# Attention with a float32 P turned by TensorE, and an order from a list scheduler, in a three-part kernel on one core

## The chip, the cores and the metric

The kernel runs on one core of one Trainium2 chip. The metric is the device time of one execution in microseconds (us); lower is better.

## What is computed

Three layers follow one another. The first is attention with rotary positions: 4 batches, 8 heads, 576 positions, 64 numbers a head. The second (called `moe` in the code) mixes each row with the row before it and squares a ReLU. The third (`moe2`) multiplies one half of a hidden layer by a normalised other half that was mixed over the positions.

```python
scores = scale * np.matmul(q_rot, k_rot.transpose(0, 1, 3, 2))
scores = scores - np.max(scores, axis=-1, keepdims=True)
attn = np.exp(scores)
attn = attn / (np.sum(attn, axis=-1, keepdims=True) + 1e-09)
attn_out = np.matmul(attn, v)
...
xk = mu_k * x + (1.0 - mu_k) * x_prev          # xr the same with mu_r
k = np.maximum(xk @ w_k, 0.0)
v = k * k @ w_v
x = v / (1.0 + np.exp(-(xr @ w_r)))
...
h = np.maximum(x @ w_in, 0.0)
u, v = h[..., :512], h[..., 512:]
v_n = (v - mean(v)) / np.sqrt(var(v) + 1e-06)
v_s = np.einsum('ts,bsd->btd', w_spatial, v_n) + b_spatial[None, :, None]
out = (u * v_s) @ w_out
```

## The kernel before

**Units of attention.** Heads go in pairs (16 of them, NP = 4 to a batch). A unit m is one block of 128 query rows of both heads of a pair; every fifth block of a pair has only 64 rows, and those of two pairs share a unit. So 72 units cover all, 18 to a batch; one in nine is such a shared unit. For each unit `scores` makes two PSUM tiles `s` (two banks each) by float32 products of `rot` (q and k after `rope`); each float32 product of the source shows as two MATMUL rows in the trace, so an ordinary unit has 8 rows and a shared one 16. Then come, for each of the two heads j: `top` (the negated row maximum, VectorE), `expo` (exp with row sums, ScalarE, into the float32 tile `pf`), and, after `norm` (1/sum), `high` and `low`, which write the normalised P as a float16 value and a float16 remainder (ScalarE and VectorE, tile `p`). `turn` transposes both by one DMA from SyncE (`pt<-p`). `values` multiplies the turned pieces with v, itself held as float16 value and remainder: 36 float16 products (72 in a shared unit) into `pv`. `gather` copies `pv` to the row tile `xt`, which is also stored to memory (`x_dram`).

**v before its use.** For each pair `v_max` takes the largest |v| (VectorE, then `partition_all_reduce` on GpSimd), `v_scale` makes scales from it, `v_split` the two float16 pieces, `v_copy` two moves by DMA. q and k are loaded through GpSimd's queue (L162).

**The first layer after attention.** Of each batch, and of each half h of its positions, `mix` makes the mixed input as two float32r pieces, `k_dot` 8 groups of 12 float32r products (tile `mk`), `k_square` the squared ReLU and its two pieces, `v_dot` 4 groups of 24 products (tile `mv`), `v_out` the copy and store to `v_dram`. That is 384 float32r products of 288 columns for a batch. The 16 pieces of the weights `w_k` and `w_v` arrive as 64-bit numbers, which `weight64` turns into float32r pieces by ScalarE, VectorE and GpSimd (L98 to L117).

**The second phase** (from L452 on) does the rest for the four batches (tiles `r`, `hv`, `u`, `sp`, `o`); its weights go through `weight64` too. Its pools open when the attention's and the first phase's close.

**Order.** An agenda of slots (two to a unit) and keys sets in which order the first phase is written out; the framework may still move instructions of an engine, as the trace shows for L223. The first `moe` work of a batch comes `LAG + 6` slots after the batch's last unit.

Of the kernel before, what the change touches and what calls it, by code (L numbers as in the profile page):

```python
# [11 lines left out]
F16 = mybir.dt.float16  # L12
# [6 lines left out]
NP = H // 2  # L19
# [4 lines left out]
NKC = 9  # L24
NFC = DF // 128
NX = NXV = 33
LATE_W = True
NFIRST = 2
WB, GB, WB2, GB2 = 5, 3, 3, 2
LAG = 8  # L30
EARLY = 0
PRE = 13
K_N, K_T, K_H, K_E, K_L = 1, 2, 3, 4, 5
K_M, K_V = 40, 10
RAW, ROT, PFS, P16S, PTS, XTS = 3, 6, 4, 3, 3, 6
P_SCALE = 2.0 ** 14


def raw(ap):
    return ap.bitcast(F32)  # L40


@with_exitstack
def body(ctx: ExitStack, tc, qp, kp, vp, cs, mu_k, mu_r, w_k, w_v, w_r, w_in, w_sp, b_sp, w_out, out):
# [8 lines left out]
    xpool = ph1.enter_context(tc.tile_pool(name="xpool", bufs=1))  # L53
    st0 = ExitStack()
    stage = [st0.enter_context(tc.tile_pool(name="st0", bufs=1)), WB, GB]
    att = ExitStack()
    at = att.enter_context(tc.tile_pool(name="att", bufs=1, side="right"))
    st0p = ExitStack()

    ps_x = st0p.enter_context(tc.tile_pool(name="ps_x", bufs=1, space=PSUM))  # L60
    ps_s = att.enter_context(tc.tile_pool(name="ps_s", bufs=2, space=PSUM, side="right"))
    ps_pv = att.enter_context(tc.tile_pool(name="ps_pv", bufs=1, space=PSUM, side="right"))
# [3 lines left out]


    cst = at.tile([128, 2, S], F32, name="cst")
    nc.sync.dma_start(cst, cs)

    mix4 = const.tile([128, NP, 4], F32, name="mix4")
    nc.sync.dma_start(mix4[:, :, 0], mu_k.rearrange("(c p) -> p c", p=128))
    nc.sync.dma_start(mix4[:, :, 2], mu_r.rearrange("(c p) -> p c", p=128))
    for k in (0, 2):
        nc.vector.tensor_scalar(mix4[:, :, k + 1], mix4[:, :, k], -1.0, 1.0, op0=ALU.mult, op1=ALU.add)
    epsc = const.tile([128, 2], F32, name="epsc")
    nc.vector.memset(epsc[:, 0:1], 1e-6)
    nc.vector.memset(epsc[:, 1:2], -0.5)
    warm = const.tile([128, 1], F32, name="warm")
    musc = const.tile([128, B, NP, 4], F32, name="musc")  # L80

    def new_stage(tag):
        n = 512 if tag != "ww" else 1160 if "p2" in pool else 1024
        return stage[0].tile([128, n], I32, tag=tag, bufs=stage[1 if tag == "ww" else 2], name=nc.get_next_instruction_name())

    def weight64(dram, r, hi, lo, c):  # L90
# [5 lines left out]
        def load():  # L96
            t["w"] = new_stage("ww")[:, :1024].rearrange("p (a b) -> p a b", b=2)
            nc.sync.dma_start(t["w"], src)  # L98

        def scale():  # L100
            lo, up = (t["w"][:, :, k] for k in range(2))
            t["g"] = t["x"] = new_stage("wg")
            nc.scalar.mul(t["g"].bitcast(F32), up.bitcast(F32), 2.0 ** -112)
            nc.scalar.mul(lo, lo.bitcast(U32), 2.0 ** -29)
            nc.vector.tensor_scalar(up, up, -2 ** 31, None, op0=ALU.bitwise_and)

        def shift():
            nc.vector.scalar_tensor_tensor(t["x"], t["g"], 3, t["w"][:, :, 1], op0=ALU.logical_shift_left,
                                           op1=ALU.bitwise_or)
# [3 lines left out]

        def low():
            x = t["x"].bitcast(F32)
            nc.scalar.copy(hi, x)
            nc.gpsimd.tensor_tensor(lo, x, raw(hi), op=ALU.subtract)  # L117

        return load, scale, shift, rest, low
# [15 lines left out]

    HEAD = slice(0, 64), slice(64, 128)

    agenda = []

    def add(slot, key, fn):  # L140
        agenda.append((slot, key, len(agenda), fn))

    def steps(gen, slots, key):
        for s in slots:
            add(s, key, lambda: next(gen, None))

    UN = 9 * NP
    preps = {}
    xt = {}

    def prep(i, s):

        b, p = divmod(i, NP)
        t = {}

        def load(which, part):
            if part == 0:
                t["raw", which] = at.tile([128, 2, S], F32, tag="raw", bufs=RAW, name=f"raw{i}_{which}")
            if i == 0:
                nc.sync.dma_start(t["raw", which][:, part, :], (qp, kp)[which][b, p, :, part, :])  # L160
            elif part == 0:
                nc.gpsimd.dma_start(t["raw", which], (qp, kp)[which][b, p])  # L162

        def rope(which):
            x = t.pop(("raw", which))
            y = t[which] = at.tile([128, S], F32, tag="rot", bufs=ROT, name=f"rot{i}_{which}")
            nc.vector.tensor_tensor(x, x, cst, op=ALU.mult)  # L167
            nc.vector.tensor_tensor(y, x[:, 0, :], x[:, 1, :], op=ALU.add)

        def v_load():  # L170
            t["vr"] = at.tile([128, 10, D], F32, tag="vr", bufs=1, name=f"vr{i}")
            nc.sync.dma_start(t["vr"], vp[b, p])

        def v_max():
            vm = t["vm"] = at.tile([128, 4], F32, tag="vm", bufs=2, name=f"vm{i}")
            nc.vector.tensor_reduce(vm[:, 0:1], t["vr"], axis=AX.XY, op=ALU.max, apply_absolute_value=True)
            nc.gpsimd.partition_all_reduce(vm[:, 1:2], vm[:, 0:1], channels=128, reduce_op=bass_isa.ReduceOp.max)
# [195 lines left out]
    def moe1(b, s):  # L373
# [5 lines left out]
        for h in range(2):  # L379
            for fc in range(NFC):  # L380
# [5 lines left out]
                if fc % 2:  # L386
                    steps(g, (m + 2,), 1.6)
# [293 lines left out]
```

## Time and profile before

| | |
|---|---|
| median of 3 runs | 937.1 us (934.18 to 942.13) |
| profiled execution: span from first to last instruction | 938.4 us |
| TensorE (PE) busy with matmuls | 796.6 us, 85% |
| VectorE (DVE), ScalarE (ACT), GpSimd (POOL) busy | 583.1, 464.0, 144.0 us |
| mean granted TensorE clock | 0.921 of 2.4 GHz |
| DMA packets under 512 bytes | 172705 of 198321 |

For the profiled execution no time beside its span is listed. A busy PE is not a PE at its peak, since rows of matmuls overlap; rates are read from how many rows start in a stretch.

### The profile page before, as it was taken

The page shows a single profiled execution, that of the slowest core. Times are in us where ns is not written, and L with a number is a line of the kernel's source. Part 1 is how long each engine was busy: PE and PEld are TensorE (multiplying, and loading weights), DVE is VectorE, ACT ScalarE, POOL GpSimd, SP SyncE. Part 2 cuts the span into 40 slices and gives each one's busy share as a digit, 9 for nine tenths or more (in the row PEclk, how much of TensorE's full clock was granted, in tenths as well). Part 3 has the DMA queues.
Part 4 walks back from the last instruction along what each step waited for, and adds up shares of the span by engine and source line. Part 5 has one row for each costly group of instructions (what it writes and reads, how often), then busy time and mean ns, then how long its engine had stood idle before and what let it go on. Part 6 is the DMA issues. An engine that isn't in the chain of part 4 may idle for free. (4 is left out here: it accounts for less than half of the span.)

```text
span 938.4 us, 16942 instructions
## 1 busy us (share of the span) xinstructions
PE 796.6 (85%) x6872; PEld 663.8 (71%) x6872; DVE 583.1 (62%) x1031; ACT 464.0 (49%) x900; POOL 144.0 (15%) x185
## 2 busy tenths in 40 slices
PE   1322478766999999898999999999989999999998
PEld 1111245444677776686777878998979999999998
DVE  3667496676688685687686785596485633254401
ACT  1525365545565563565675775576273442253311
POOL 1525360000000000000000000246160100010000
PEclk9999756557599999899999999999999999999999
DMA  7449587676497689777766758543532020200001
GB/s 277 150 113 149 137 171 133 153 164 157 88 186 177 110 152 128 145 169 167 139 115 149 147 116 139 156 142 127 167 119 77 1 101 13 89 14 26 26 27 51
DMA packets 198321, 114.20 MB, mean 122 GB/s; under 512 B 172705, under 2 KB 176801, under 8 KB 198242
## 3 DMA queue, kind: packets, MB, share of 16 engines
q1 hardware_dynamic: 191618, 90.69, 44.7%
q0 software_dynamic: 4320, 17.70, 6.4%
q10 hardware_dynamic: 2304, 4.73, 1.7%
q8 instruction: 54, 0.88, 0.4%
q14 instruction: 25, 0.20, 0.1%
HBM read 52.26 MB, written 14.16 MB: 71 GB/s over the span
## 5 line engine op out<-in xcount | busy, mean ns | idle before, releaser
L223 PE MATMUL s<-rot,rot 64*128 64x288 f32 (+1 forms) x640 | 200.7, 516 | 107.8 <-ACT pf L235 92.3
L223 PEld LDWEIGHTS s<-rot,rot 64*128 64x128 f32 (+1 forms) x640 | 103.5, 214 | 159.2 <-ACT pf L235 108.4
L235 ACT ACTIVATE pf<-s,sm 128x576 f32<-128x576 f32 x144 | 106.1, 738 | 100.2 <-DVE sm L230 93.9
L277 PEld LDWEIGHTS <-vv 128*64 128x64 f16 x2880 | 92.5, 123 | 60.1 <-issue 59.2
L251 DVE SCALAR_TENSOR_TENSOR p<-pf,sm,p 128x576 f16<-128x576 f32 x144 | 115.8, 829 | 30.5 <-ACT p L247 30.1
L247 ACT ACTIVATE p<-pf,sm 128x576 f16<-128x576 f32 x144 | 103.7, 767 | 46.9 <-DVE sm L241 17.3
L277 PE MATMUL pv<-pt,vv 128*64 128x128 f16 (+1 forms) x2880 | 109.7, 235 | 20.0 <-DMA pt<-p 20.0
L335 PE MATMUL mk<-x,wk 128*128 128x288 f32 x768 | 121.6, 307 | 3.1 <-DVE rl L346 2.8
L335 PEld LDWEIGHTS mk<-x,wk 128*128 128x128 f32 x768 | 106.2, 192 | 19.1 <-issue 8.6
L364 PE MATMUL mv<-kh,wv 128*128 128x288 f32 x512 | 116.4, 310 | 0.0
L230 DVE TENSOR_REDUCE sm<-s 128x1 f32<-128x576 f32 x144 | 106.5, 748 | 11.1 <-PE s L223 11.0
L364 PEld LDWEIGHTS mv<-kh,wv 128*128 128x128 f32 x512 | 86.8, 194 | 10.7 <-issue 8.4
L364 PE MATMUL mv<-kl,wv 128*128 128x288 f32 x256 | 77.7, 304 | 1.4 <-DVE kl L352 1.4
L167 DVE TENSOR_TENSOR raw<-raw,cst 128x1152 f32<-128x1152 f32 x32 | 44.2, 1383 | 40.3 <-DMA raw<-qp 25.2
L452 PE MATMUL r<-xr,wr 128*128 128x288 f32 x384 | 55.9, 301 | 3.3 <-DVE xr L456 2.5
L452 PEld LDWEIGHTS r<-xr,wr 128*128 128x128 f32 x384 | 53.4, 193 | 4.4 <-DVE xr L456 2.9
L452 PE MATMUL sp<-ws,vn 128*128 128x288 f32 x384 | 53.9, 295 | 0.0
L452 PE MATMUL o<-g,wo 128*128 128x288 f32 x384 | 53.0, 296 | 0.5 <-ACT os L582 0.5
L452 PE MATMUL u<-x,wi 128*128 128x288 f32 x384 | 53.2, 296 | 0.0
L452 PEld LDWEIGHTS u<-x,wi 128*128 128x128 f32 x384 | 52.4, 188 | 0.9
L452 PEld LDWEIGHTS sp<-ws,vn 128*128 128x128 f32 x384 | 52.4, 188 | 0.7
L452 PEld LDWEIGHTS o<-g,wo 128*128 128x128 f32 x384 | 51.7, 188 | 1.4 <-ACT os L582 1.2
(325 smaller groups left out, 973.8 us busy)
## 6 DMA issues: line engine op xcount, KB each, us to landing
raw<-kp POOLq DMA_DIRECT2D x15, 576.0 KB, 7.5
raw<-qp POOLq DMA_DIRECT2D x15, 576.0 KB, 6.1
vr<-vp SPq DMA_DIRECT2D x16, 320.0 KB, 3.6
xd<-xt ACTq DMA_DIRECT2D x16, 288.5 KB, 4.6
vd<-vs SPq DMA_DIRECT2D x32, 144.0 KB, 1.8
v<-vd SPq DMA_DIRECT2D x16, 288.0 KB, 2.8
out<-os SPq DMA_DIRECT2D x16, 288.0 KB, 2.1
vv<-vv SPq DMA_DIRECT2D x32, 128.0 KB, 2.9
```

Of the source, the lines that this page charges most:

```text
L167: nc.vector.tensor_tensor(x, x, cst, op=ALU.mult)
L223: nc.tensor.matmul(o, q[r, 128 * c:min(128 * c + 128, S)], k[r, h * HALF:(h + 1) * HALF], start=True, stop=True)
L230: nc.vector.tensor_reduce(sm[:, 0, j:j + 1], ps[j], axis=AX.XY, op=ALU.max, negate=True)
L235: nc.scalar.activation(pf[j].rearrange("p (a b) -> p a b", a=2), ps[j], AF.Exp, bias=sm[:, 0, j:j + 1], scale=1.0, accum_out=sm[:, 1, j:j ...
L247: nc.scalar.mul(p16[:, j, 0, :], pf[j], sm[:, 3, j:j + 1])
L251: nc.vector.scalar_tensor_tensor(p16[:, j, 1, :], pf[j], sm[:, 3, j:j + 1], p16[:, j, 0, :], op0=ALU.mult, op1=ALU.subtract)
L277: nc.tensor.matmul(o, preps[i]["vv"][:, kc, j, D * hl:D * hl + D], a, start=kc + hl == 0, stop=kc + hl == NKC)
L335: nc.tensor.matmul(ps[:, :HALF], wk[w][:, c, fc * 128:(fc + 1) * 128], a[:, c, :], start=m == 0, stop=m == 11)
L364: nc.tensor.matmul(ps[:, :HALF], wv[w][:, fc, dc * 128:(dc + 1) * 128], a, start=m == 0, stop=m == 23)
L452: nc.tensor.matmul(ps[:, h, :HALF], w, a[:, h * HALF:(h + 1) * HALF], start=m == 0, stop=m == n - 1)
```

## The change

P stays float32 and is not divided by its row sum before it is turned. TensorE turns it with an identity matrix, 4 blocks of 128 columns into one PSUM bank (`turn`, n = 0 and 1, one for each head) and a last block of the two heads' remaining columns together with the broadcast reciprocals of the sums (n = 2). `take` copies these three to SBUF, two on ScalarE and one on VectorE. `values` is then 10 float32 products of 64 by 128 with the unsplit v, and `gather`, now on VectorE, multiplies by the turned reciprocals while leaving PSUM. In shared units P is normalised first (`scaled`) and `gather` copies. v's maximum, scales, split and moves go, and with them `partition_all_reduce` and the `musc` scales. q and k are loaded by SyncE, `v_out` moves to ScalarE, the square of the ReLU becomes one product of 576 columns for two groups.

The whole first phase, the weights, and the first loads and weights of the second phase become steps of a `Plan`: each has an engine, an estimated duration, dependencies and a rank, and `order` takes at each point the step that can begin first. It is written out in that order, which nothing moves afterwards. Scores of a unit are one step for both heads, with the heads' products alternating, and wait for both exps of the unit before. The moe products go in pieces of 6. Two PSUM banks are shared by moe products and `values` (`m`), two serve `turn`. The buffers of weights go from 5 and 3 to 3 and 2, and the second phase has 4 instead of 3 of the PSUM tiles of `hv`.

```diff
+    def order(self):
+        free = dict.fromkeys(("PE", "ACT", "DVE", "POOL", "SP"), 0.0)
...
+                for s in steps:
+                    if any(d.end is None for d in s.deps):
+                        continue
+                    t = max([free[e]] + [d.end + d.after for d in s.deps])
+                    if s.take:
+                        if not room[s.take]:
+                            continue
+                        t = max(t, min(room[s.take])[0])
+                    key = (t, s.rank)
...
-            nc.gpsimd.partition_all_reduce(vm[:, 1:2], vm[:, 0:1], channels=128, reduce_op=bass_isa.ReduceOp.max)
...
-                nc.gpsimd.dma_start(t["raw", which], (qp, kp)[which][b, p])
...
+                    nc.sync.dma_start(t["raw", k], (qp, kp)[k][b, p])
...
+    plan = Plan({"m": 2, "t": 2, "ww": WB, "wg": GB})
...
+        def scaled(u):
+            p = st["p"][:, u, :]
+            nc.vector.tensor_scalar(p, p, st["r"][:, u, 0:1], None, op0=ALU.mult)
+
+        def turn(n, slot):
+            pt = st["t", n] = ps_t.tile([128, 4, 128], F32, tag=f"t{slot}", name=f"t{m}_{n}")
+            p = st["p"]
...
+            elif n < 2:
+                for c in range(4):
+                    k = 64 * n + 128 * c
+                    nc.tensor.transpose(pt[:, c, :], p[:, n, k:k + 128], ident)
+            else:
+                nc.tensor.transpose(pt[:, 0, :], p.rearrange("p a b -> p (a b)")[:, 512:640], ident)
+                nc.tensor.transpose(pt[:, 1, :], st["r"].rearrange("p a b -> p (a b)"), ident)
...
+            nc.scalar.copy(o, x) if eng == "ACT" else nc.vector.tensor_copy(o, x)
...
+                for c in range(5):
+                    for j in range(2):
...
+                            a, x = (v[:, 4 * j + c, :], pt[:, 4 * j + c, :]) if c < 4 else \
+                                (v[HEAD[j], 8, :], pt[HEAD[j], 8, :])
+                        nc.tensor.matmul(o, a, x, start=c == 0, stop=c == 4)
...
+                nc.vector.tensor_tensor(rows(i)[:, 1 + 128 * c:129 + 128 * c], st["v"][:, 0:128], st["pt"][:, 9, :],
+                                        op=ALU.mult)
...
+        scored[m] = s = add("PE", 1.95 if tail else 1.0, scores, need + [exps.get((m - 1, j)) for j in range(2)], m - 1.0)
+        mx = [add("DVE", 0.75, lambda j=j: top(j), [s], m - 0.6) for j in range(2)]
...
+            turned[m, n] = add("PE", (0.4, 0.4, 0.25, 0.1)[n], lambda slot, n=n: turn(n, slot), ready[n], m + 0.1 * n, take="t")
+            eng = ("ACT", "ACT", "DVE", "DVE")[n]
...
+        v = valued[m] = add("PE", 1.0, values, ev + [vloads[i] for i, _ in w], m + 0.9, take="m")
...
+            z = add("PE", 0.79, lambda slot, k_dot=k_dot: k_dot(0, slot), done + wk_ready, rank(fc), take="m")
+            p = add("PE", 0.79, lambda k_dot=k_dot: k_dot(1), [z], rank(fc) - 1)
...
-        nc.vector.tensor_copy(vs, ps[:, :HALF])
+                nc.scalar.copy(vs, xs["v", dc][:, :HALF])
...
+    close = add("SP", 0.0, open_second, over, 74, 0.1)
...
+    with tc.manual_schedule():
+        plan.emit()
...
-    ps1 = ctx.enter_context(tc.tile_pool(name="ps1", bufs=3, space=PSUM, reuse_waits="tile"))
+    ps1 = ctx.enter_context(tc.tile_pool(name="ps1", bufs=4, space=PSUM, reuse_waits="tile"))
```

## Rows read from the trace of the kernel before

**Rows 1.** The page: span and busy us (share of the span) of each engine.

```profile
span 938.4 us, 16942 instructions
...
PE 796.6 (85%) x6872; PEld 663.8 (71%) x6872; DVE 583.1 (62%) x1031; ACT 464.0 (49%) x900; POOL 144.0 (15%) x185
```

**Rows 2.** Windows of all engines: stretch, its us, busy us (instructions) each, clock, DMA.

```profile
15.00:190.00 175.00, 91.53 (x666) 56.93 (x667) 117.44 (x184) 84.29 (x165) 58.31 (x53) 0.78 0.65 146
...
400.00:570.00 170.00, 165.15 (x1766) 130.20 (x1760) 130.31 (x255) 107.66 (x226) 7.00 (x17) 0.99 0.69 141
570.00:669.00 99.00, 94.51 (x886) 90.39 (x883) 64.41 (x102) 55.89 (x109) 35.65 (x27) 1.00 0.49 132
```

**Rows 3.** The same windows, of L223 (scores) alone: PE and PEld.

```profile
15.00:190.00 175.00, 66.90 (x162) 33.94 (x163) 0.78 0.65 146
...
400.00:570.00 170.00, 54.62 (x232) 28.68 (x232) 0.99 0.69 141
```

**Rows 4.** Waits from 15 to 190 us: in total, times, longest.

```profile
PE s L223 <- ACT pf L235: 63.2, 15, 16.7
...
PE pv L277 <- DMA pt<-p: 20.0, 4, 13.1
...
ACT I-587_588 L103 <- POOL wk L117: 14.4, 1, 14.4
```

**Rows 5.** Timeline of POOL: start, us, what, idle before it.

```profile
58.62 0.38 POOL L177 PARTITION_ALL_REDUCE vm<-vm  x1 [6.03 <-DMA I-618_619<-w_v]
...
67.90 1.25 POOL L117 TENSOR_TENSOR wk<-I-364_365,wk 128x512 fp32r<-128x512 f32 x1 [8.28 <-issue]
```

**Rows 6.** Timeline of PE near the end of attention, at full clock.

```profile
564.95 1.24 PE L223 MATMUL s<-rot,rot 64*128 64x288 f32 x8
566.12 0.40 PE L364 MATMUL mv<-kh,wv 128*128 128x288 f32 x1
...
567.90 1.20 PE L277 MATMUL pv<-pt,vv 128*64 128x128 f16 x36
569.03 1.24 PE L223 MATMUL s<-rot,rot 64*128 64x288 f32 x8
```

**Rows 7.** Timeline of all engines from 428 us: scores of one head alone.

```profile
427.88 1.23 PE L223 MATMUL s<-rot,rot 64*128 64x288 f32 x4
```

**Rows 8.** Single lines: ns of one row (min/median/max), first and last start.

```profile
L223 PE MATMUL s<-rot,rot x640: 402/403/846, 15.2 to 569.9; 64*128 64x288 f32 x128, 64*64 64x288 f32 x32
...
L277 PE MATMUL pv<-pt,vv x2880: 196/219/317, 57.1 to 594.0; 128*64 128x128 f16 x152, 128*64 128x64 f16 x40
...
L335 PE MATMUL mk<-x,wk x768: 289/295/610, 247.5 to 654.5; 128*128 128x288 f32 x192
```

**Rows 9.** Groups by line and shape: count, busy us, mean ns, idle before.

```profile
L251 DVE SCALAR_TENSOR_TENSOR p<-pf,sm,p 128x576 f16<-128x576 f32 x144 | 115.8, 829 | 30.5 <-ACT p L247 30.1
L230 DVE TENSOR_REDUCE sm<-s 128x1 f32<-128x576 f32 x144 | 106.5, 748 | 11.1 <-PE s L223 11.0
...
L235 ACT ACTIVATE pf<-s,sm 128x576 f32<-128x576 f32 x144 | 106.1, 738 | 100.2 <-DVE sm L230 93.9 <-DVE p L251 4.7 <-DVE sm L241 1.2
L247 ACT ACTIVATE p<-pf,sm 128x576 f16<-128x576 f32 x144 | 103.7, 767 | 46.9 <-DVE sm L241 17.3 <-ACT pf L235 15.3 <-issue 11.4
...
L235 ACT ACTIVATION_READ_ACCUMULATOR pf<-s,sm 128x1 f32 x144 | 27.9, 194 | 0.0
...
L291 ACT COPY xt<-pv 128x512 f32<-128x512 f32 x16 | 9.2, 574 | 3.1 <-PE pv L277 3.1
```

**Rows 10.** Timeline of PE: the first phase's last product and the second's start.

```profile
668.10 0.29 PE L364 MATMUL mv<-kh,wv 128*128 128x288 f32 x1
668.23 6.41 PE L452 MATMUL r<-xr,wr 128*128 128x288 f32 x48
```

**Rows 11.** Windows 570 to 669 us: PE, PEld and ACT of `r`; PE and PEld of `mk`.

```profile
570.00:669.00 99.00, 8.90 (x54) 7.86 (x55) 1.30 (x2) 1.00 0.49 132
...
570.00:669.00 99.00, 42.14 (x288) 38.78 (x288) 10.81 (x24) 9.62 (x24) 1.00 0.49 132
```

More of the change, by code (lines that the diff above doesn't have):

```diff
@@ L433, in body @@
[L433 to L439 removed]
+        return [(2 * g, 4), (2 * g + 1, 4)] if w == 4 else [(2 * g + w // 5, w % 5 if w < 4 else w - 5)]
@@ new lines, in body @@
+    for c in range(16):
+        k = c < 8
+        args = (w_k, c // 2, wk[0][:, c // 2], wk[1][:, c // 2], c % 2) if k else (w_v, c - 8, wv[0][:, c - 8], wv[1][:, c - 8], 0)
+        (wk_ready if k else wv_ready).append(weight_steps(lambda args=args: args, 1.1 * c + (0 if k else 6)))
+    for m in range(NU):
+        for i, _ in which(m):
+            while i not in ropes:
+                prep(len(vloads))
+        unit(m)
+        for i in range(B * NP):
+            if i not in ropes and i >= ROT // 2 and max(which_last(i - 3)) <= m:
+                prep(i)
+        if m % 18 == 17:
+            if m == NU - 1:
+                over = list(plan.steps)
+            for h in range(2):
+                feed(m // 18, h)
@@ new lines, in body, with open_second @@
+    second = {}
+    st2 = ExitStack()
+    def open_second():
+        att.close()
+        p2 = second["p2"] = ctx.enter_context(tc.tile_pool(name="p2", bufs=1, side="right", reuse_waits="tile"))
+        second["wr"] = [p2.tile([128, NP, DM], F32R, tag=f"wr{i}", name=f"wr{i}") for i in range(2)]
+        second["wi"] = [p2.tile([128, NP, DF], F32R, tag=f"wi{i}", name=f"wi{i}") for i in range(2)]
+        second["xr"] = [p2.tile([128, NP, S], F32R, tag=f"xr{i}", name=f"xr{i}") for i in range(2)]
+        stage[:] = st2.enter_context(tc.tile_pool(name="st2", bufs=1, side="right", reuse_waits="tile")), WB2, GB2
@@ new lines, in mix_steps, with load, parts, first @@
+    def mix_steps(c, r, old):
+        t = {}
+        def load(slot):
+            t["x"] = new_stage("ww", slot).bitcast(F32)
+            nc.sync.dma_start(t["x"][:, :S + 1], x_dram[0][:, c, :])
+        def parts():
+            x = t["x"]
+            return x[:, :S], x[:, 1:S + 1], x[:, S + 1:2 * S + 1], second["xr"][0][:, c, :], second["xr"][1][:, c, :]
+        def first():
+            a, _, y, _, _ = parts()
+            nc.scalar.mul(y, a, mix4[:, c, 3:4])
+        def then():
+            _, a, y, _, _ = parts()
+            nc.vector.scalar_tensor_tensor(y, a, mix4[:, c, 2:3], y, op0=ALU.mult, op1=ALU.add)
+        def high():
+            _, _, y, hi, _ = parts()
+            nc.scalar.copy(hi, y)
+        def low():
+            _, _, y, hi, lo = parts()
+            nc.vector.tensor_tensor(lo, y, raw(hi), op=ALU.subtract)
+        s = x = add("SP", 0.4, load, [old], r - 1, 3.5, take="ww")
+        for eng, us, fn in (("ACT", 0.7, first), ("DVE", 0.75, then), ("ACT", 0.7, high)):
+            s = add(eng, us, fn, [s], r)
+        add("DVE", 0.75, low, [s], r, give=x)
@@ L614, in body @@
         gate(b)
-        if b == 0 and not LATE_W:
-            more_weights()
-            st2.close()
-            p4 = ctx.enter_context(tc.tile_pool(name="p4", bufs=1, side="right", reuse_waits="tile"))
         if b % 2:
```

631 lines of the change are left out of this document (325 added, 306 removed).

## The prediction

> **What bounds the kernel now.** The page comes first: PE is busy for 85% of the span [rows 1]. That is an average over stages with different limits, so the windows by stage come next, then the waits and the timeline inside each. The scores line serves as the clock of the first phase: 18 units show 160 of its rows (16 ordinary units of 8, two shared ones of 16).
>
> From the first scores at 15.2 us [rows 8] to 190 us the trace has 162 rows, so 18 units take 175 us, 9.7 us each [rows 3]. There PE is busy for half of the time, at a mean granted clock of 0.78, VectorE for two thirds, ScalarE for half [rows 2]: nothing is full, and the chain stalls. The waits name its links [rows 4]: scores wait 63.2 us for exps, up to 16.7 us at once; products with v wait 20 us for the transposing DMA; ScalarE once stands 14.4 us behind a weight step of GpSimd. The timeline of POOL shows why GpSimd was late: around the partition_all_reduce, 0.38 us of work, it sits idle for 6.03 us before and, after one DMA issue, 8.28 us "issue" behind it [rows 5]. ScalarE executes in order, so exps stand behind a weight step that waits for GpSimd, and scores behind the exps.
>
> The last scores start at 569.9 us [rows 8]; so the other 54 units take 380 us, 7.0 us each. From 400 to 570 us PE is busy for 165.15 of 170 us [rows 2]; 232 score rows at 8.9 a unit are 26.1 units, 6.5 us each [rows 3]. This stage is bound by PE. Its bill for a unit: scores 54.62 / 26.1 = 2.09 us; products with v 1.13 us, from one group's start to the next's (567.90 to 569.03) [rows 6]; moe 384 / 18 = 21.3 products at 1.78 / 12 = 0.148 us (566.12 to 567.90) [rows 6], 3.16 us. Sum 6.38, against 165.15 / 26.1 = 6.33.
>
> From 570 to 669 us PE still does the 288 + 288 moe products left over (the `mk` row shows 288; the `mv` ones are the other half, as the split of 8 groups of 12 and 4 of 24 makes equal) and 54 of `r` [rows 11]. The second phase proper runs from 668.23 us to the end, 270 us [rows 10, 1].
>
> **Part by part: PE in the stage that it bounds.** Scores: the four rows of one head alone occupy 1.23 us [rows 7], the eight of both heads 1.24 us, 1.17 to the next group [rows 6]. Two heads side by side cost what one does. Before, the framework mostly kept them apart (2.09 us a unit); the change writes them alternating, nothing moves them, and both tiles are awaited first. So 1.17, and with eight more rows in a shared unit, 1.28 on average: 0.81 less.
>
> A float32 row of 288 columns shows 402 ns, a float32r row 295 [rows 8]; float32r rows start every 6.41 / 48 = 0.134 us [rows 10], so I estimate 0.134 + 0.107 = 0.24 us for a float32 row. Four of these are 0.96, which leaves 0.21 of the 1.17 as the change-over between kinds of products. For 128 columns the float32 row is 0.107 us.
>
> Products with v: 10, so 20 rows, in pairs that use different halves of the output. Pairs do run together: the 36 float16 rows take 1.13 us, 0.031 each, while 128 columns alone at the float32r rate are 0.060. So 10 x 0.107 + 0.21 = 1.28 us, 0.15 more; ends 1.13 (nothing dearer than now) and 2.35 (no pairing).
>
> Turning is new on PE and no row shows it: 10 blocks of 128 by 128 a unit. Lower end 0.060 us each, one pass of 128 columns; upper end 0.214, a full float32 product, two rows. Within one pass, loading 128 columns of weights is hidden in the 0.134 us of a float32r product, so it costs at most that. I take the middle of 0.060 and 0.134, 0.095, since each block is loaded as weights and used once, and one change-over: 1.15 us. With three change-overs the ends are 0.8 and 2.77.
>
> The page "TensorE: Matmul & The Clock Gate", Part 4, of the Trainium skill puts one such transpose at some 275 ns inside a kernel, though for bf16. No row here is a transpose; the float16 rows with v last 219 ns each [rows 8] and yet follow every 31, so a row's length isn't its price in a stream. By that figure the sum would be 1.8 us a unit more and the whole near 995 us.
>
> Moe keeps its products: 3.16 us. Sum 1.28 + 1.28 + 1.15 + 3.16 = 6.9 us a unit, against 7.0 now. What pairing gives, turning takes. 54 x 6.9 = 373 us.
>
> The other engines have room under 6.9 us. VectorE now has 130.31 / 26.1 = 5.0 us a unit, ScalarE 107.66 / 26.1 = 4.1 [rows 2]. VectorE loses two `low` of 0.829 [rows 9] and the work on v, and gains a copy, the scaling gather and a broad reciprocal, each at most the 0.574 of a copy of 512 columns [rows 9]: about 4 to 5. ScalarE loses two `high` of 0.767 and gains two copies of 0.574 [rows 9] and the copies of `v_out`: about 4. The chain of a unit is scores 1.17, two maxima of 0.748, the last exp with its sum read 0.738 + 0.194 [rows 9], some 0.3 of hand-overs: 3.9 us, also under 6.9, and moe pieces fill PE meanwhile.
>
> **The first 18 units.** Here go the two GpSimd gaps of each all-reduce, the wait on the transposing DMA, the work on v and its two moves on SyncE. The lower bound is the chain, 3.9 us a unit; PE's bill without moe is 1.28 + 1.28 + 1.15 = 3.7 us at full clock but 7.4 at half, and this stage has a mean of 0.78 now [rows 2]. The upper bound is today's 9.7. Weights still load ScalarE, VectorE and GpSimd, and ScalarE still waits in order for GpSimd's part. I take 6.0: between the chain and PE at half clock. 18 x 6.0 = 108 us, against 175. The start stays at 15 us: the same loads of cos/sin, q and k come first. They go to SyncE's queue, which no longer holds transposes but now orders loads behind stores of `xt` and `vs`; the loads are asked for nine units early, which covers that. If that cover goes, VectorE waits for q and k, and I count it with the second rival.
>
> **The end of the first phase.** Moe of a batch may start as soon as its rows are there, not `LAG` + 6 slots later, so behind the last unit stands one batch, 384 x 0.134 = 51 us, plus some 9 for the last unit's own chain and mix: 60 us, against 99 now. The second phase's weights are loaded and split in these 60 us; today they share the 99. The steps wait until all of attention and the third batch's moe is done, so this cover is thinner, but PE has 51 us of products meanwhile.
>
> **The second phase** keeps its products. Its 54 `r` products that now run inside the first phase's tail come back, 54 x 0.134 = 7 us: 277. A fourth PSUM tile for `hv` I cost at nothing, PE being full there.
>
> **Sum.** 15 + 108 + 373 + 60 + 277 = 833 us, against the span of 938.4. The median of the runs is 1.3 lower than that span, so 832. The gain is 67 us in the first 18 units, 7 in the stage that PE bounds, 39 - 7 at the end.
>
> **The rivals.** (a) *PE is cheaper than my bill.* Change-overs hide and a transpose is 0.060: scores 1.1, v 1.13, turning 0.8, moe at 0.134 a product 2.86, so 5.9 to 6.0 a unit; first units 4.6. 15 + 83 + 324 + 58 + 272 = 752. For: contiguous moe rows do follow at 0.134 [rows 10]. Against: every change of kind in rows 6 costs its 0.2, and the change makes more of them.
>
> (b) *The fixed order stalls.* PE's order was made from estimates that differ from the trace (scores 1.0 against 1.17, six products 0.79 against 0.89), and two banks serve moe and v, so that a ReLU that is late on ScalarE halts PE with everything behind it. A stall of 1.2 us a unit, about one exp and its hand-over, and 1.0 us in the first 18: 833 + 65 + 18 = 916. Against: PE is the engine that is underestimated, so the others tend to be ahead.
>
> (c) *The first units stay slow.* If the stalls came from weights and not from the all-reduce and the DMA, they stay at 9.7 us: 833 + 67 = 900. Then the change doesn't do what its removals say. Against: rows 5.
>
> (d) *Turning costs full float32 products.* Place: PE, each unit. 10 x 0.214 and three change-overs are 2.77 us, 1.62 more in 54 units (87 us) and twice that at half clock in 18 (58): 978, slower than before. It decides from an excess e with 54 e + 36 e = 105, e = 1.2 us a unit, or 2.3 us for the turning of a unit. For: the data are float32, and float32 products show two rows each [rows 8]. Against: nothing is accumulated or rounded in a turn.
>
> **How the numbers follow.** Chances: forecast 0.51, (a) 0.18, (b) 0.15, (c) 0.08, (d) 0.08. The range leaves out (d) and the outer halves of (a) and (b): 755 to 915. A per cent, about 9 us, is what a measurement here tells from no change. Faster: the forecast, (a), (c) and most of (b), 0.87. Within a per cent: what of (b) and (d) lies there, 0.05. Slower: (d), 0.08.
>
> **What would show it.** In the new trace: first scores near 15 us, the 19th unit's near 123, the last unit's near 496, the last `mv` near 556. Eight score rows together in about 1.2 us at full clock; 20 rows with v in 1.3; ten turns in 1.15 with their change-over. PE busy above 0.95 between 150 and 490 us, and no gaps of 6 to 8 us on POOL. The prediction is wrong if PE waits there for ScalarE or VectorE (b), if a turn follows the next by 0.2 us (d), or if the first 18 units take over 150 us (c).

## The result and the profile after

The changed kernel takes 861.9 us in the median of 4 runs (861.05 to 862.86), beside 935.73 us for the kernel before on the same chip: a ratio of 0.9205, with a 95% interval of 0.9169 to 0.9241. The forecast was 832 us, its range 755 to 915. The direction holds, the time lies in the range, and the forecast is 30 us too low.

The page of the kernel after, answering [rows 1], and from its groups of instructions the ones that are new or changed most (count, then busy us and mean ns of one, then idle time ahead):

```profile
span 859.9 us, 15505 instructions
...
PE 798.0 (93%) x6392; PEld 687.0 (80%) x6392; DVE 545.8 (63%) x933; ACT 432.9 (50%) x884; POOL 115.5 (13%) x127
...
L327 PE MATMUL v<-pt,vt 128*64 128x128 f32 (+3 forms) x1600 | 119.2, 279 | 3.1 <-DVE pt L310 1.0
L261 PE MATMUL s<-rot,rot 64*128 64x288 f32 (+1 forms) x640 | 106.3, 444 | 12.1 <-DVE rot L225 12.0
...
L297 PE MATMUL t<-ident,pf 128*128 128x128 f32 x512 | 83.7, 288 | 6.2 <-ACT pf L271 5.3
...
L278 DVE RECIPROCAL rb<-sm 128x128 f32<-128x128 f32 x72 | 68.6, 953 | 2.5
```

PE is busy for as long as before (798.0 against 796.6 us) in a span that is 78.5 us shorter: the gain is idle time of PE that went. Busy time alone would not show that, nor that the mean granted clock rose from 0.921 to 0.973, so the windows by stage are read next, cut where the stages of after lie; they answer to [rows 2]. Columns: us, then busy us (instructions) of PE, PEld, DVE, ACT and POOL, then granted clock, DMA share, GB/s.

```profile
12.00:130.00 118.00, 94.51 (x732) 62.99 (x733) 103.64 (x171) 73.92 (x157) 41.84 (x33) 0.87 0.46 147
...
150.00:500.00 350.00, 349.34 (x3188) 289.32 (x3186) 248.72 (x451) 192.68 (x434) 0.79 (x8) 1.00 0.17 53
500.00:591.00 91.00, 80.93 (x610) 77.57 (x607) 53.40 (x66) 50.22 (x99) 37.81 (x27) 0.96 0.37 112
```

The kernel before had in its middle stage, from the 19th unit's first scores to the last unit's:

```profile
189.30:570.00 380.70, 351.36 (x3564) 269.22 (x3564) 277.90 (x529) 222.35 (x464) 20.53 (x49) 0.91 0.73 145
```

The windows of after for the scores line L261 alone count the units, 160 rows to 18 units as in [rows 3]; the columns are PE and PEld, clock, DMA:

```profile
0.00:130.00 130.00, 33.34 (x160) 17.86 (x160) 0.88 0.49 160
130.00:500.60 370.60, 72.65 (x480) 39.86 (x480) 1.00 0.17 55
```

With the first score at 12.0 us, the last at 500.5 and the last `mv` row at 589.4, the stages stand so (us):

| stage | before | forecast | after |
|---|---|---|---|
| up to the first scores | 15 | 15 | 12 |
| first 18 units | 175 | 108 | 118 |
| 54 units | 380 | 373 | 370.5 |
| last scores to last `mv` | 99 | 60 | 89 |
| the rest | 270 | 277 | 270 |
| sum | 938 | 833 | 860 |

Of the 27 us that the sum is short, 29 are the end of the first phase and 10 the first 18 units; the other three lines are 3, 2.5 and 7 us shorter than forecast.

PE's timeline in the middle stage prices the kinds, beside [rows 6, 7]. Columns: start, us, operation, rows in a run.

```profile
301.83 0.66 PE L297 MATMUL t<-ident,pf 128*128 128x128 f32 x4
302.24 0.38 PE L459 MATMUL mv<-kh,wv 128*128 128x288 f32 x1
...
303.21 1.24 PE L261 MATMUL s<-rot,rot 64*128 64x288 f32 x8
304.38 0.40 PE L459 MATMUL mv<-kh,wv 128*128 128x288 f32 x1
...
306.52 0.27 PE L299 MATMUL t<-ident,pf 128*128 128x128 f32 x1
306.63 0.27 PE L300 MATMUL t<-ident,rb 128*128 128x128 f32 x1
...
308.07 1.46 PE L327 MATMUL v<-pt,vt 128*64 128x128 f32 x20
309.46 1.24 PE L261 MATMUL s<-rot,rot 64*128 64x288 f32 x8
```

Starts are what counts, not lengths. Eight score rows: 303.21 to 304.38, 1.17 us, as forecast. The 20 rows with v: 308.07 to 309.46, 1.39, forecast 1.28. Four turns 0.41 to the next kind, and one turn 0.11 after another: a turn is one row of 0.27 us that costs a PE at work 0.11.

### The profile page after: what moved, and what is told of

Its sections match the earlier page's. It is cut to its first block, busy times and chain, and to the rows that moved or that the text cites. A ratio compares the mean times of both kernels' runs of the same rounds, so it can differ in the third digit from the quotient of the medians.

```text
span 859.9 us, 15505 instructions
## 1 busy us (share of the span) xinstructions
PE 798.0 (93%) x6392; PEld 687.0 (80%) x6392; DVE 545.8 (63%) x933; ACT 432.9 (50%) x884; POOL 115.5 (13%) x127
## 4 chain that ended last, share of the span: by engine, by line
PE 78%; DVE 11%; ACT 4%; DMA 3%; issue 2%; POOL 1%; SPq 0%; DVEq 0%; ACTq 0%; POOLq 0%
PE mv L459 11%; PE v L327 11%; PE mk L419 10%; PE s L261 9%; PE sp L590 7%; PE t L297 7%; PE o L590 6%; PE r L590 5%; PE u L590 5%; PE hv L654 5%; DVE raw L224 2%; DVE sm L266 2%; DVE rb L278 1%; DMA mix<-mu_k 1%; DVE rot L225 1%
## 5 line engine op out<-in xcount | busy, mean ns | idle before, releaser
L310 ACT COPY pt<-t 128x512 f32<-128x512 f32 x144 | 83.6, 586 | 103.0 <-PE t L297 84.9
L266 DVE TENSOR_REDUCE sm<-s 128x1 f32<-128x576 f32 x144 | 106.2, 748 | 31.5 <-PE s L261 30.4
L459 PE MATMUL mv<-kh,wv 128*128 128x288 f32 x512 | 119.3, 309 | 7.3 <-ACT vs L465 6.1
L327 PE MATMUL v<-pt,vt 128*64 128x128 f32 (+3 forms) x1600 | 119.2, 279 | 3.1 <-DVE pt L310 1.0
L261 PE MATMUL s<-rot,rot 64*128 64x288 f32 (+1 forms) x640 | 106.3, 444 | 12.1 <-DVE rot L225 12.0
L419 PE MATMUL mk<-x,wk 128*128 128x288 f32 x768 | 115.8, 301 | 1.7 <-ACT rl L426 1.7
L327 PEld LDWEIGHTS v<-pt,vt 128*64 128x64 f32 (+1 forms) x1600 | 85.0, 140 | 34.6 <-issue 19.0
L419 PEld LDWEIGHTS mk<-x,wk 128*128 128x128 f32 x768 | 103.6, 188 | 6.3 <-ACT rl L426 2.2
L297 PE MATMUL t<-ident,pf 128*128 128x128 f32 x512 | 83.7, 288 | 6.2 <-ACT pf L271 5.3
L261 PEld LDWEIGHTS s<-rot,rot 64*128 64x128 f32 (+1 forms) x640 | 57.7, 184 | 37.5 <-DVE rot L225 12.0
L297 PEld LDWEIGHTS t<-ident,pf 128*128 128x128 f32 x512 | 58.6, 144 | 31.7 <-issue 19.4
L278 DVE RECIPROCAL rb<-sm 128x128 f32<-128x128 f32 x72 | 68.6, 953 | 2.5
```

The costliest lines, as they stand in the source:

```text
L261: nc.tensor.matmul(o, q[r, 128 * c:min(128 * c + 128, S)], k[r, h * HALF:(h + 1) * HALF], start=True, stop=True)
L266: nc.vector.tensor_reduce(st["sm"][:, 0, j:j + 1], st["s"][j][:, :, :HALF], axis=AX.XY, op=ALU.max, negate=True)
L278: nc.vector.reciprocal(r, sm[:, 2, :].unsqueeze(2).to_broadcast([128, 2, D]))
L297: nc.tensor.transpose(pt[:, c, :], p[:, n, k:k + 128], ident)
L310: nc.scalar.copy(o, x) if eng == "ACT" else nc.vector.tensor_copy(o, x)
L327: nc.tensor.matmul(o, a, x, start=c == 0, stop=c == 4)
```

## The experiments

Every ratio is against the kernel before on the same chip, with its 95% interval. Kernels whose medians are compared with one another without that ran on different occasions, so differences of 3 or 4 us between them are left undecided.

### Where PE's time in the middle stage goes

**Heads written one after the other.**

```diff
-                for h in range(2):
-                    for j in range(2):
+                for j in range(2):
+                    for h in range(2):
```

> Scores of a unit are issued head after head again (all rows of one head, then all of the other); everything else, the order too, as in the changed kernel. If TensorE bounds the middle 54 units, an ordinary unit costs 8 x 0.24 + 0.21 = 2.13 us in place of 1.17 and a shared one 2 x 0.96 more, 1.07 on average: 54 x 1.07 = 58 us more, about 920 us, and the middle stage goes from 370 to about 428 us; the first 18 units change little. If the fixed order's stalls on the other engines set the middle stage, TensorE has slack and under 20 us are added.

Measured: 861.0 us, 0.9167 (0.9101 to 0.9232), no different from after. The timeline shows why: PE still takes all 8 rows in the time that 4 took before (1.25 us here, 1.23 in [rows 7]).

```profile
303.57 1.25 PE L261 MATMUL s<-rot,rot 64*128 64x288 f32 x8
```

My reading that the alternation makes the pairing falls. Four rows of one head and then four of the other run side by side as well, so long as nothing else is queued between them. The edit therefore took nothing away, and the worth of pairing needed another kernel:

**One turn of the identity between the two heads' rows** (ordinary units only).

```diff
-                for h in range(2):
-                    for j in range(2):
+                for j in range(2):
+                    if j == 1 and not tail:
+                        nc.tensor.transpose(ps[0][:, 1, 384:512], ident, ident)
+                    for h in range(2):
```

> In ordinary units one transpose of the identity stands between the score rows of the first head and those of the second, so that the two groups can't run beside each other; its result is used by nobody. If running side by side is what makes 8 rows cost 1.17 us, the second group of 0.96 comes on top, with the transpose (0.11) and two change-overs: 1.2 to 1.4 us in 48 ordinary units of the middle stage, which grows from 370 to about 430 us, and the whole to 915 to 930. If the rows don't overlap, only the transpose and its change-overs come on top, 0.3 to 0.5 us a unit: about 880.

Measured: 940.99 us, 1.0024 (0.9965 to 1.0083): the whole gain is gone. The timeline in the same stage:

```profile
305.72 1.24 PE L263 MATMUL s<-rot,rot 64*128 64x288 f32 x4
306.88 0.33 PE L259 MATMUL s<-ident 128*128 128x128 f32 x1
307.14 1.24 PE L263 MATMUL s<-rot,rot 64*128 64x288 f32 x4
308.30 0.66 PE L299 MATMUL t<-ident,pf 128*128 128x128 f32 x4
...
144.00:580.80 436.80, 435.13 (x3385) 340.81 (x3382) 268.88 (x483) 207.58 (x464) 5.93 (x15) 1.00 0.15 47
```

One small row between the heads makes 2.58 us (305.72 to 308.30) of 1.17. Over 48 ordinary units that is 48 x 1.41 = 68 us; the stage, from the 19th unit's first scores at 144.2 to the last score at 580.6 us, is 436 us long against 370.5, so 66 longer. The first 18 units take 14 us more. The pairing is shown, and so is its price.

**Every turn twice.**

```diff
-                        nc.tensor.transpose(pt.rearrange...
+                        for _ in range(2): nc.tensor.transpose(pt.rearrange...
```
(and the same in the three other calls)

> Every transpose of P is issued twice into the same place. If a transpose costs its spacing of about 0.11 us and TensorE bounds the middle stage, 10 x 0.11 = 1.1 us a unit are added: 54 x 1.1 = 59 us in the middle, 0 to 20 in the first 18 units, 920 to 940 us in all. If a transpose costs a full float32 product (0.214 us), 116 us or more are added. If TensorE has slack, under 20 us.

Measured: 929.08 us, 0.9899 (0.9838 to 0.9959). The first 18 units take about 129 us, the next 54 about 425, 55 more than in after:

```profile
300.21 1.09 PE L297 MATMUL t<-ident,pf 128*128 128x128 f32 x8
...
141.00:567.00 426.00, 424.48 (x3929) 360.78 (x3927) 267.03 (x482) 206.57 (x464) 6.09 (x15) 1.00 0.15 48
```

That is 55 / 54 = 1.02 us a unit. The window has 591 rows more than that of after (3929 against 3338; an ordinary unit has ten turns, a shared one twenty smaller ones), so a turn costs 0.09 us on average. PE is busy for 424.48 of 426 us at a granted clock of 1.00: everything added to PE there is paid in full, so PE bounds the stage. Rival (d), 0.214 a turn, is refuted.

**The order not fixed** (the framework may move instructions again).

```diff
-    with tc.manual_schedule():
-        plan.emit()
+    plan.emit()
```

> The plan is written out as before, but the framework may move instructions of an engine again. If the gain comes from the work that is left out and from paired scores, and the fixed order only keeps the pairs, this loses what unpairing costs (up to 58 us) and stays under 925 us; if the scheduler's order itself carries the gain, it falls back to 930 us or more; if the framework keeps or betters the order, 850 to 865 us.

Measured: 912.12 us, 0.9772 (0.9728 to 0.9816). In the timeline moe rows stand between the two heads again, each head 1.16 us to the next kind:

```profile
313.91 1.23 PE L261 MATMUL s<-rot,rot 64*128 64x288 f32 x4
315.07 1.85 PE L419 MATMUL mk<-x,wk 128*128 128x288 f32 x12
316.85 1.24 PE L261 MATMUL s<-rot,rot 64*128 64x288 f32 x4
```

The 54 units run from about 137 us to the last score at 551.5, 414 against 370.5. So 50 of the 74 us that the change brings need the fixed order, 44 of them in this stage. PE is busy in it for 412.87 of 413.8 us, so it is not waiting: its work costs more. In after the rows of a unit stand together in every one of the 54 units but one; here they come in 102 runs, 50 of them of 4 rows and 22 shorter. Leaving a unit's score rows together is thus most of what the fixed order does; that other changes of kind cost nothing more here was not tested apart.

### What the first 18 units wait for

**The kernel before without its all-reduce.** This kernel puts the constant 0.6 where the maximum over partitions was, so that v's scales are no longer those of the data.

```diff
-            nc.gpsimd.partition_all_reduce(vm[:, 1:2], vm[:, 0:1], channels=128, reduce_op=bass_isa.ReduceOp.max)
+            nc.gpsimd.memset(vm[:, 1:2], 0.6)
```

> The kernel before, with a constant 0.6 in place of the largest |v| over all partitions: the partition_all_reduce on GpSimd is left out, the rest stays. If its gaps on GpSimd held up the first 18 units (175 us), these take some 140 to 155 us and the whole 20 to 35 us less than before, so 900 to 916. If the first units wait for the transposing DMA and for the chain of exps anyway, less than 8 us are gained.

Measured: 899.49 us, 0.9592 (0.9524 to 0.966). The first 18 units run from 15.5 to 154.7 us, 139 against 175, though at a lower granted clock, 0.66 for 0.78 [rows 3]. The scores line in that window, and the wait that led [rows 4]:

```profile
15.50:154.70 139.20, 67.50 (x160) 34.58 (x160) 0.66 0.74 182
...
PE s L223 <- ACT pf L235: 38.4, 17, 8.5
```

Of the 57 us that the change gains in this stage, 36 come with the all-reduce, whose own row is 0.38 us long [rows 5]: what it costs is the idle time about it, as the prediction had it. The wait of scores for exps falls from 63.2 to 38.4 us, and the waits of ScalarE for GpSimd together from 40 to 8. The middle stage gets 9 us shorter as well (372 for 381). The other 21 us belong to the rest of what was removed there and were not split.

**The reciprocal on two columns, then a broad copy.**

```diff
-            nc.vector.reciprocal(r, sm[:, 2, :].unsqueeze(2).to_broadcast([128, 2, D]))
+            nc.vector.reciprocal(sm[:, 3, :], sm[:, 2, :])
+            nc.vector.tensor_copy(r, sm[:, 3, :].unsqueeze(2).to_broadcast([128, 2, D]))
```

> The reciprocal is taken of two numbers a row and then copied out to 128 columns, in place of a reciprocal of 128 columns that takes 0.953 us: VectorE has about 0.6 us a unit less to do, the order stays. If VectorE bounds the first 18 units, these get 18 x 0.6 = 11 us shorter and the middle stage keeps its 370 us: about 851 us. If the first units hang on weights or GpSimd, nothing changes (862). If VectorE, not TensorE, sets the middle stage, 30 to 43 us are gained in all.

Measured: 858.94 us, 0.9153 (0.9098 to 0.9207); its first 18 units take 118 us like those of after. The reason is in VectorE's groups of the first stage, 12 to 130 us:

```profile
L279 DVE COPY rb<-sm 128x128 f32<-128x128 f32 x18 | 10.9, 606 | 0.6
L278 DVE RECIPROCAL sm<-sm 128x2 f32<-128x2 f32 x18 | 3.0, 166 | 0.6
```

The copy that stood in for the reciprocal (0.953 us) has a mean of 0.606 there, though later in the same trace its longest of 50 is 0.230. So hardly anything was taken from VectorE: it is busy for 100.6 us of this stage, against 103.6 in after. Something stretches rows of VectorE while the weights come in, and the timeline of after, VectorE and GpSimd beside each other, says what:

```profile
30.38 1.80 POOL L160 TENSOR_TENSOR wk<-I-137_138,wk 128x512 fp32r<-128x512 f32 x1 [0.75 <-ACT wk L157]
...
31.18 2.22 DVE L224 TENSOR_TENSOR raw<-raw,cst 128x1152 f32<-128x1152 f32 x1
32.15 2.39 POOL L154 TENSOR_TENSOR I-217_218<-I-217_218,I-117_118 128x512 int32<-128x512 int32 x1
33.43 1.72 DVE L225 TENSOR_TENSOR rot<-raw 128x576 f32<-128x576 f32 x1
...
35.27 0.95 DVE L278 RECIPROCAL rb<-sm 128x128 f32<-128x128 f32 x1
```

Beside weight steps of GpSimd L224 takes 2.22 us and L225 1.72; from 150 us on, their means are 1.335 and 0.758 (GpSimd is busy there for 0.79 us up to 500). The reciprocal keeps its 0.95 beside GpSimd. The theory is now: GpSimd's weight steps hold VectorE, and VectorE holds the first 18 units. The rival: the stage is held by ScalarE's order and the loads, and VectorE only looks busy.

**GpSimd's weight steps made small.** Of `w_k` and `w_v` GpSimd handles 8 of 512 columns and clears the low piece instead of computing it; `w_r` and `w_in` are set to zero and neither loaded nor split. So the results of all layers behind attention are left out.

```diff
-            nc.gpsimd.tensor_tensor(t["x"], t["x"], t["w"][:, :, 0], op=ALU.add)
+            z = 8 if dram is w_k or dram is w_v else 512
+            nc.gpsimd.tensor_tensor(t["x"][:, :z], t["x"][:, :z], t["w"][:, :z, 0], op=ALU.add)
...
-            nc.gpsimd.tensor_tensor(lo, t["x"].bitcast(F32), raw(hi), op=ALU.subtract)
+            if dram is w_k or dram is w_v:
+                nc.gpsimd.memset(raw(lo), 0.0)
...
+    for k in ("wr", "wi"):
+        for i in range(2):
+            add("POOL", 3.0, lambda k=k, i=i: nc.gpsimd.memset(raw(second[k][i]), 0.0), [close], 76)
```

> Two stages are read from this run, and its output isn't the reference's. For w_k and w_v GpSimd's two steps of 512 columns are left out but for 8 columns and a clearing of the low piece. And the loads and splitting of w_r and w_in at the end of the first phase are left out, both are set to zero. First stage: if VectorE, held up by GpSimd's steps (a copy of 0.228 us takes up to 1.18 there), sets it, the 118 us fall to 105 to 110; if TensorE and the chain of the unit set it, they stay within 3 us. End of the first phase: if the weights on ScalarE, VectorE and GpSimd lengthen it, it falls from 89 to 72 to 78 us (434 products x 0.134, 6 of the last units, little idle time, no r rows inside); if moe's own chain through two PSUM banks does, PE keeps its 10 us of idle time.

Measured: 838.32 us, 0.8926 (0.8872 to 0.8981). VectorE's groups in the first 18 units, of after (12 to 130 us) and then of this kernel (10.8 to 119 us), and this kernel's windows of that stage and of the end of the first phase:

```profile
L224 DVE TENSOR_TENSOR raw<-raw,cst 128x1152 f32<-128x1152 f32 x10 | 16.6, 1660 | 0.0
L278 DVE RECIPROCAL rb<-sm 128x128 f32<-128x128 f32 x17 | 16.2, 953 | 0.6
L225 DVE TENSOR_TENSOR rot<-raw 128x576 f32<-128x576 f32 x10 | 11.4, 1142 | 0.3
...
L276 DVE TENSOR_SCALAR sm<-sm 128x2 f32<-128x2 f32 x17 | 5.8, 341 | 0.4 <-ACT pf L271 0.4
```

```profile
L282 DVE RECIPROCAL rb<-sm 128x128 f32<-128x128 f32 x17 | 16.2, 953 | 0.6
L228 DVE TENSOR_TENSOR raw<-raw,cst 128x1152 f32<-128x1152 f32 x10 | 13.4, 1337 | 0.0
L229 DVE TENSOR_TENSOR rot<-raw 128x576 f32<-128x576 f32 x10 | 7.6, 758 | 0.3
...
L280 DVE TENSOR_SCALAR sm<-sm 128x2 f32<-128x2 f32 x17 | 2.7, 161 | 0.4 <-ACT pf L275 0.4
...
10.80:119.00 108.20, 90.55 (x730) 60.72 (x730) 92.29 (x171) 74.52 (x157) 13.68 (x33) 0.91 0.51 165
488.70:567.10 78.40, 77.24 (x608) 74.91 (x604) 25.54 (x42) 29.42 (x61) 10.24 (x6) 1.00 0.15 48
```

With the same 171 instructions VectorE is busy for 92.29 us instead of 103.64, 11.4 less, 10.1 of them in the three groups that differ; the stage is 109 us instead of 118. What VectorE gains the stage gains, as the theory wants, and the waits bear it out: those of PE for VectorE, after the first scores, fall from 17.1 to 9.6 us, those for ScalarE rise from 5.4 to 6.8. The rival isn't shut out by this run alone, since the same edit takes ScalarE's waits for GpSimd from 5.1 to 0.9 us; and a part of the gain may come by way of the granted clock, 0.87 in after and 0.91 here. The run with the broad copy on ScalarE, below, leaves GpSimd's work as it was. The reciprocal is 953 ns in both, and beside GpSimd's clearing of memory (MEMSET, 0.52 us) L229 keeps its 0.76.

The Trainium skill, "SBUF — State Buffer", section "Who interferes with whom", says that VectorE shares one pair of SBUF ports with GpSimd: instructions with two SBUF inputs contend with a GpSimd instruction that reads SBUF, copies and scalar operations may, and one-input instructions outside the two-port modes do not. The trace agrees: L224 and L225 stretch, the copy and L276 too, and the reciprocal doesn't (953 ns beside GpSimd as without it).

**The same with the narrow reciprocal** (leaves out what the last one does; edit as above).

> As the run with the light GpSimd steps (the same parts are left out), with the narrow reciprocal as well. If VectorE sets the first stage and the narrow form gained nothing only since its copies waited for GpSimd, 18 x 0.6 = up to 11 us more are gained in the first stage. If not, it is as without it.

Measured: 833.7 us, 0.8882 (0.8829 to 0.8934). The 19th unit's scores start at 116.2 us, so the first 18 take 105 us, 3 less again. VectorE falls from 92.3 to 86.0 us (10.8 to 117), not by the 11 that the rows unstretched would give, since the broad copy still has a mean of 373 ns: twelve of the 18 take 226 to 229 ns, the six others, each beside a clearing of memory by GpSimd, 368 to 1021. So a copy is stretched also by what only writes on GpSimd, which two-input rows are not. The stage follows VectorE's gain by about a half. So VectorE held this stage only until it was relieved by some 11 us; what holds the last 105 us was not settled. PE is then busy for 91.23 of 106.2 us at a granted clock of 0.90.

### What lengthens the end of the first phase

The timeline of after at the one long wait of PE in this stage:

```profile
534.50 1.70 POOL L154 TENSOR_TENSOR I-5811_5812<-I-5811_5812,I-5750_5751 128x512 int32<-128x512 int32 x1 [1.22 <-ACT x L396]
534.96 3.01 DVE L399 TENSOR_TENSOR x<-mf,x 128x288 fp32r<-128x288 f32 x2
...
536.24 0.62 ACT L157 CAST wr<-I-5811_5812 128x512 fp32r<-128x512 f32 x1 [1.63 <-POOL I-5811_5812 L154]
...
537.89 1.94 DVE L390 SCALAR_TENSOR_TENSOR mf<-xt,mix,mt 128x288 f32<-128x288 f32 x2
539.43 0.86 ACT L396 CAST x<-mf 128x288 fp32r<-128x288 f32 x2 [2.58 <-DVE mf L390]
...
542.45 0.68 ACT L465 COPY vs<-mv 128x288 f32<-128x288 f32 x2
...
542.89 0.61 PE L459 MATMUL mv<-kh,wv 128*128 128x288 f32 x1 [6.07 <-ACT vs L465]
543.29 0.44 PE L459 MATMUL mv<-kl,wv 128*128 128x288 f32 x1
```

Read from below: PE stands 6.07 us until ScalarE has copied `mv` out of its bank. That copy is no slower than others (0.68 us for two rows, 0.40 for one in the median), but it stands in order behind weight steps and mixes of the second phase. These wait: 1.63 us for GpSimd, 2.58 for VectorE, whose two rows of L399 take 3.01 us beside GpSimd (0.89 for the next two, where GpSimd is idle). So all three engines are late through work of the second phase, and behind the wait PE's rows last half as long again (0.44 for 0.29): from 543 to 547 us the granted clock is 0.50, its lower level of 1.2 GHz, after it was 1.00 before the wait.

With GpSimd's steps light and those weights zero (second of the two windows shown of that kernel), this stage is 78.4 us instead of 89.2, although PE does 96 rows of `r` in it against 83. PE is idle for 1.2 us instead of 10.1, and its only wait there is one of 1.1 us for a ReLU. The second phase's weights in the same stage are what the 10 us are, their loads and their steps together (the DMA share falls too, from 0.37 to 0.15); moe's own chain through two banks, the rival, is worth 1.

**The second phase's weights after the first phase** (opened and loaded behind it in the program).

```diff
-            weight_steps(...)
...
+    opened()
+    for k, c, q in todo:
+        ...
+            load64(w_in, c, wi[0][:, c], wi[1][:, c], q)
```

> The second phase's first weights and inputs (the steps on w_r, x and w_in) are taken out of the plan and written out behind it. If sharing ScalarE, VectorE and GpSimd with these steps made the end of the first phase longer (89 us from the last scores to the last mv product, forecast 60), it falls to about 66 us (434 moe products x 0.134 and 8 for the last unit), while the weights then stand bare: about 40 us before the first hv products, so the whole comes out 10 to 25 us slower, 872 to 887. If the end is long for another reason (moe's own chain ReLU, square, split), it stays near 80 to 89 us and the whole is 30 us or more slower.

Measured: 865.05 us, 0.9269 (0.9224 to 0.9314). Inconclusive: the weight steps ran among the moe steps all the same, on ScalarE from 517 us on, and the last `mv` came at 594.3 us. They were not where the experiment wanted them, so it tells neither theory.

### A better order

**Measured durations in the list scheduler**, the trace's numbers in place of the estimates (scores 1.17 for 1.0, products with v 1.4 for 1.0, the reciprocal 1.16 for 0.39, and so on), alone and with the narrow reciprocal.

```diff
-... 1.95 if tail else 1.0, scores ...
+... 2.15 if tail else 1.17, scores ...
-... add("DVE", 0.39, norm ...
+... add("DVE", 1.16, norm ...
```

> The plan gets the durations that the trace of the changed kernel shows (scores 1.17, v 1.4, turns 0.5, 0.5, 0.25, the reciprocal 1.16 in place of 0.39, rope 2.35, GpSimd's weight steps 1.6 and a few more); the instructions are the same. If wrong estimates made stalls in the first 18 units and at the end, 5 to 20 us are gained (842 to 857). If these stages are bound by VectorE and by the chains themselves, it stays within 4 us of 862.

Measured: 857.92 us, 0.9189 (0.9148 to 0.9231).

> The narrow reciprocal and the measured durations (0.6 for it) together. If both theories hold, 11 us in the first units and 5 to 15 from the order: 836 to 846 us. If only VectorE's load counts, about 851.

Measured: 855.1 us, 0.9165 (0.9116 to 0.9214). Neither interval is apart from that of after: what better numbers give the scheduler is a few us at most. By stage they shift time: with measured durations alone the end of the first phase takes 80 us instead of 89 (with 45 rows of `r` in it for 83, which is 5 of the 9), but the first 18 units 123 instead of 118 and the middle 373. Rival (b), stalls of 1.2 us a unit, is out by after itself, where PE is busy for 349.34 of 350 us. Its mechanism, a late ScalarE that keeps a bank of the two, does appear in the 6.07 us above, but at the end of the phase and through the weights.

**The broad copy on ScalarE**, with the narrow reciprocal on VectorE and measured durations. ScalarE is the less busy of the two in every window.

```diff
-            nc.vector.reciprocal(r, sm[:, 2, :].unsqueeze(2).to_broadcast([128, 2, D]))
+            nc.vector.reciprocal(sm[:, 3, :], sm[:, 2, :])
+        def spread():
+            r = st["r"] = at.tile([128, 2, D], F32, tag="rb", bufs=3, name=f"rb{m}")
+            nc.scalar.copy(r, st["sm"][:, 3, :].unsqueeze(2).to_broadcast([128, 2, D]))
```

> An attempt at a faster version: measured durations in the plan, the reciprocal of two numbers a row on VectorE, copied out to 128 columns by ScalarE. If VectorE sets the first stage, it gets 5 to 10 us shorter and the whole comes to 846 to 852; if the order and not VectorE's load counts there, it stays near the 855 of the two edits together.

Measured: 849.71 us, 0.9053 (0.8999 to 0.9107), the fastest version that computes everything; its interval lies below that of after. The window that counts its first 160 score rows:

```profile
0.00:124.00 124.00, 30.86 (x160) 16.45 (x160) 0.89 0.51 168
```

The 19th unit's scores start at 126.0 us; from the first score at 10.7 that is 115 us for the first 18 units. Beside the run before it (narrow reciprocal and measured durations, copy on VectorE: 122 us) the stage is 6.5 us shorter and VectorE in it busy for 95.8 us instead of 104.4, with GpSimd as busy as there (46 us in both). So here too the stage follows VectorE, with GpSimd's work untouched. The other stages: 366 us for 54 units (last score at 492.5) and 85 to the last `mv` at 577.4.

## Why the prediction was right, and where it was off

**The first 18 units.** The mechanism holds: the gaps about the all-reduce alone were 36 us of this stage. The value chosen, 6.0 us a unit, measured 6.6; it was picked between 3.9 and 7.4 and not added up, so that it came so near is in part luck. Rival (c) is refuted. What the step passed over is VectorE: costed with rows of 400 to 570 us, where GpSimd hardly works, while here its rows are stretched by 11 us. Without that stretch the stage took 109 us, so the missing 10 us are worth about these; how much of them came through ScalarE's waits or the clock was not split. That VectorE stayed the fullest engine (103.64 of 118 us) also has a cause that was priced wrongly: "a broad reciprocal, each at most the 0.574 of a copy" measured 0.953. In the middle stage this price changed nothing: the narrow reciprocal left it at 370 us, and VectorE is busy there for 248.72 of 350.

**PE in the middle stage.** 373 us forecast, 370.5 measured, 6.86 us a unit for 6.9; rival (a), 5.9 to 6.0, is out. Scores were 1.17 as forecast. Products with v were 1.39 for 1.28. A turn was 0.09 for 0.095, which was only a middle between two bounds and right by chance as much as by reason. (Of these bounds for a unit, 2.77 us has three change-overs in it and 0.8 only one.) The 275 ns of the Trainium skill, "TensorE: Matmul & The Clock Gate", Part 4, would have cost 1.8 us a unit more; the rows do last 0.27 to 0.29 us and the price is 0.09, so here too the length of a row in a stream isn't its cost. The stated reason for the pairing was wrong in part: not the alternation, but nothing between the heads. And the nearness of the sum is in part an offset: it has 1152 moe products in this stage, 48 more than ran there (below), 48 x 0.148 = 7 us too many, against 6 us too few for the products with v (54 x 0.11).

The 380 us of before weren't all PE's, either. The 165.15 of 170 us that the prediction read belong to 400 to 570 us; over the whole stage PE was idle for 29 of 381 us, at a granted clock of 0.91. In after it is idle for 3 of 370, at 1.00, and does 1104 moe products there for 960. So what shortened this stage is the idle time and the clock, while what a unit costs PE rose, as the sum had it (6.38 us by its bill, 6.86 measured).

**The end of the first phase: the step that failed.** "60 us" was 51 of products, 9 of a chain, and a cover that would hide the weights: "PE has 51 us of products meanwhile". It measured 89. Three parts:

- 83 rows of `r` ran inside, 83 x 0.134 = 11 us. The prediction had put all of `r` behind this stage, so this is only moved: the second phase is 270 us, not 277.
- One batch was not all that stood behind the last unit. From 500.5 us on there are 192 rows of `mk` and 240 of `mv`, 432 instead of 384: 48 x 0.134 = 6 us.
- The weights were not hidden. PE was idle for 10.1 us and ran at 0.96 of its clock; with the weight work mostly gone the same stage lost 10.8 us, though 13 more rows of `r` (2 us) ran in it, so the weights cost some 12. The prediction wrote "this cover is thinner" and then priced that at nothing. It had to be read on ScalarE, VectorE and GpSimd, through which both moe and the weights go, and not on PE, which covers nothing that it waits for itself.

Together 11 + 6 + 12 = 29 us, the 29 that were missing, if the 9 of the chain are taken as they were.

**The second phase.** It measured 270 us. With the 11 us of `r` that ran before it, it would be 281 against the 277 of the forecast; these 4 us are unexplained.

## What to carry to other kernels

Where TensorE is full, price by starts, not by lengths or busy time, and look what stands between two groups that could run side by side: one small row between them cost more here (1.4 us a unit) than all the turns of a unit (1.0). Work is hidden only if every engine that it passes through has room, in order: list for a cover which engines both sides use, and what the covering engine itself waits for. A duration is to be taken from a stretch in which the same neighbours work; VectorE's rows with two inputs take a quarter to a half longer here in a stage with GpSimd's weight steps than in one without, and its reciprocal takes the same.

## What the hardware showed that was not expected

- Two heads' score rows overlap without being alternated, and a single 128-column turn between them ends the overlap: 1.17 us become 2.58.
- The reciprocal takes 953 ns for 128 columns, the copy of the same tile 227; a reciprocal of 2 columns takes 166.
- L224 goes from 1.337 to 1.660 us in the mean and L225 from 0.758 to 1.142 with GpSimd at its weight steps, and a scalar operation on 2 columns from 161 to 341 ns. Clearing memory on GpSimd left rows with two inputs as they were (758 ns), but stretched six copies from 227 to between 368 and 1021 ns.
